# A routed FFN in slots of four blocks instead of two, and the last product scaled in its bank behind both branches

## The chip, the cores and the metric

One core of a Trainium2 chip runs the whole program. The metric is the device time of one execution in microseconds (us). TensorE (PE) does the matrix products, VectorE (DVE), ScalarE (ACT) and GpSimd (POOL) the rest, SyncE (SP) and POOL issue transfers. Each engine takes its instructions in program order.

## What is computed

Attention (4 batches, 8 heads, 768 tokens, each over its near neighbours and block summaries) gives x, 3072 rows of 512. Then each row goes through one of eight experts:

```
logits = x @ w_gate; local_gate = sigmoid(x @ w_local)
e = argmax(logits) if s == 0 or local_gate < 0.5 else the row before's e
p = softmax(logits)
out = p[e] * (max(x @ w1[e], 0) @ w2[e])      # w1 512x1024, w2 1024x512
```

## The kernel before

Rows are sorted by expert into 128-row blocks, numbered 0 to 25 here. With these inputs blocks 0 to 5 are batch 0 (one expert, known early, so they start while attention still runs), 6 to 16 belong to one expert (17 is empty), 18 to 23 to another, 24 to a third (25 is empty). Two "few" blocks of 32 rows take small rests of experts, in single fp32 products with unsplit weights ("raw").

A pair slot does two blocks. A gather on POOL fetches a block's rows, four transposes on PE and a cast and a subtraction on ACT and DVE (`tx`, `split_ps`) make xT in two parts, high and low, since each fp32 product is done as three matmuls on parts (high x high, high x low, low x high). Weights are split likewise, by ACT for the high part and DVE or POOL for the low part. Product 1 (`pair`, L1149 to L1151) is 96 matmuls of 256 columns, both blocks side by side; ACT and DVE make hT of it (L1155, L1157). Product 2 (`mm`, L1055 to L1057) is 48 matmuls of 512 columns, 24 for each block. In product 2 stand, at steps given by tables, the transposes of the next slot's blocks (PM0 in the first slot, PM in the others) and the splits of the next weights (PW1, PW2, four chunks each; SPLIT_BY says on which engine, V for DVE).

The order of each engine's work is the order of the code. Up to block 5, a list of small steps (the routing sort of batches 1 to 3) is dealt out between the steps of the slots by a planner (`flow`); whatever of it is left when the slot ends is put there. Two of its results matter here: the words that tell SP, POOL and the other engines which experts follow (PE L978), and the probabilities by block (`bp`: DVE L990 and three of L995, then 24 matmuls L999 on PE, then DVE L1002). Engines read words into registers with loads that their own sequencers run (`reg`, L1294), and branch on them. From block 14 on, each slot branches into a pair or a single. At block 22 a test on the number of blocks chooses the usual end (L1446) or a long one. The last product's rows are scaled by DVE and ACT, half each, and scattered (`last_rows`).

Of the kernel before, what the change touches and what calls it, by code (L numbers as in the profile page):

```python
# [19 lines left out]
P = 128  # L20
# [27 lines left out]
FEW_AT = 34  # L48
# [16 lines left out]
PM, PM0 = (2, 5), (10, 13)  # L65
# [12 lines left out]
class Kernel:  # L78
    def __init__(self, ctx, tc, qT, kT, vT, vW, maskc, identc, wgc, w1, w2, c32c, cb16c, out):
# [13 lines left out]
        self.turn = 0  # L93
# [44 lines left out]
    def bank(self, which):  # L138
        if which == "a" and "a2" in self.ps:
            self.turn ^= 1  # L140
            which = "a2" if self.turn else "a"
        return self.ps[which].tile([P, 512], F32, name="b" + which)
# [880 lines left out]

    def gather(self, i):
        t = self.xg[i % 2]
# [15 lines left out]
    def tx(self, i, half=0, bank="t"):  # L1041

        ps = self.transposes(lambda c: self.xg[i % 2][:, c, G9:G9 + P], bank).rearrange("p (k t) -> p k t", k=KT)
        self.split_ps(ps, self.xT[:, :, 0, half], self.xT[:, :, 1, half])

    def th(self, src, name):
        ps = self.transposes(lambda c: src[:, P * c:P * c + P], "t")
        h, l = [self.fw.tile([P, 512], F32R, name=name + x) for x in "hl"]
        self.split_ps(ps, h, l)
        return h, l  # L1050
# [8 lines left out]
    def store(self, yp, i, act=False, alone=False):  # L1059
        while self.have_p <= i:  # L1060
            self.small(1, True)
        if i >= LATE and (i % 2 or alone):
# [3 lines left out]
        y = self.mw2.tile([P, 512], F32, name="yo", bufs=2)  # L1066
# [17 lines left out]
    def few_rows(self, j):  # L1084

        t = self.xm[j]
        self.nc.gpsimd.indirect_dma_start(out=t.rearrange("p a d -> p (a d)"), out_offset=None, in_=self.x_rows,
                                          in_offset=bass.IndirectOffsetOnAxis(ap=self.gidx[0:FEW, SLOTS + j:SLOTS + j + 1], axis=0))

    def few_prep(self, j):  # L1090

        nc, fw, b = self.nc, self.fw, j
        i = SLOTS + j
        ps = self.bank("t")
        for c in range(KT):
            nc.tensor.transpose(out=ps[:, FEW * c:FEW * c + FEW], in_=self.xm[b][:, c, G9:G9 + P], identity=self.ident[0:FEW, 0:FEW])
        nc.vector.tensor_copy(out=self.xf[b].rearrange("p k t -> p (k t)"), in_=ps[:, 0:KT * FEW])
        rp = fw.tile([FEW, 2], F32, name="rp")
        nc.vector.tensor_copy(out=rp[:, 0:1], in_=self.sidx[0:FEW, i:i + 1])
        nc.vector.tensor_copy(out=rp[:, 1:2], in_=self.psort[0:FEW, i:i + 1])  # L1100
        yield
        ps = self.bank("t")
        nc.tensor.matmul(out=ps[:, 0:2], lhsT=self.four, rhs=rp, start=True, stop=True)
        nc.vector.tensor_scalar(out=self.idx4[b], in0=ps[:, 0:1], scalar1=4.0, scalar2=self.c["quad"], op0=ALU.mult, op1=ALU.add)
        nc.vector.tensor_copy(out=self.p4[b], in_=ps[:, 1:2])

    def few(self, j):

        nc, fw, b = self.nc, self.fw, j
        s1, s2 = self.raw  # L1110
        ps = self.bank("s")[:, 0:DF // 4]
        for k in range(KT):
            for q in range(4):
                c0 = 2 * P * (KT * q + k)
                nc.tensor.matmul(out=ps[FEW * q:FEW * q + FEW], lhsT=self.xf[b][:, k], rhs=s1[:, c0:c0 + DF // 4],
                                 start=(k == 0), stop=(k == KT - 1))
        h = fw.tile([P, DF // 4], F32, name="fh")
        nc.scalar.activation(out=h, in_=ps, func=AF.Relu)
        yield
        ps = self.bank("t")[:, 0:DF // 4]  # L1120
        for c in range(2):
            nc.tensor.transpose(out=ps[:, P * c:P * c + P], in_=h[:, P * c:P * c + P], identity=self.ident)
        hT = fw.tile([P, 2, 4, FEW], F32, name="fhT")
        nc.vector.tensor_copy(out=hT.rearrange("p c q t -> p (c q t)"), in_=ps)
        yield
        ps = self.bank("a")[:, 0:P]
        for f in range(FT):
            for q in range(4):
                c0 = f * DM + P * q
                nc.tensor.matmul(out=ps[FEW * q:FEW * q + FEW], lhsT=hT[:, f % 2, f // 2], rhs=s2[:, c0:c0 + P],  # L1130
                                 start=(f == 0), stop=(f == FT - 1))
        y = fw.tile([P, P], F32, name="fy")
        nc.vector.tensor_scalar(out=y, in0=ps, scalar1=self.p4[b], scalar2=None, op0=ALU.mult)
        nc.gpsimd.indirect_dma_start(out=self.out.rearrange("t (q d) -> (t q) d", q=4),
                                     out_offset=bass.IndirectOffsetOnAxis(ap=self.idx4[b], axis=0),
                                     in_=y, in_offset=None, bounds_check=4 * T_ALL - 1, oob_is_err=False)

    def pair(self, i, mid, w1, w2):

        nc = self.nc  # L1140
        xT, hT = self.xT, self.hT
        for f in range(0, FT, 2):
            ps = self.bank("s").rearrange("p (f t) -> p f t", f=2)
            for j in range(2):
                for k in range(KT):
                    c0 = 2 * P * (KT * (f // 2) + k) + P * j
                    xh, xl = [xT[:, k, part].rearrange("p h t -> p (h t)") for part in range(2)]
                    wh, wl = [w[0][:, c0:c0 + P] for w in (self.hi, self.lo)]
                    nc.tensor.matmul(out=ps[:, j], lhsT=wh, rhs=xh, start=(k == 0), stop=False)  # L1149
                    nc.tensor.matmul(out=ps[:, j], lhsT=wh, rhs=xl, start=False, stop=False)  # L1150
                    nc.tensor.matmul(out=ps[:, j], lhsT=wl, rhs=xh, start=False, stop=(k == KT - 1))  # L1151
                    if k % 2:
                        yield
            h, l = hT[:, f:f + 2, 0], hT[:, f:f + 2, 1]
            nc.scalar.activation(out=h, in_=ps, func=AF.Relu)  # L1155
            self.dve(0.6, self.t + 0.5)
            nc.vector.scalar_tensor_tensor(out=l, in0=ps, scalar=0.0, in1=h.bitcast(F32), op0=ALU.max, op1=ALU.subtract)  # L1157
        for half in range(2):
            yp = self.ya if half and 2 * i >= LATE else self.bank("a")
            s = slice(P * half, P * half + P)  # L1160
            for f in range(FT):
                self.mm(yp, hT[:, f, 0, s], hT[:, f, 1, s], 1, lambda t: t[:, f * DM:f * DM + DM], f == 0, f == FT - 1)
                yield
                j = FT * half + f
                pm = PM if i else PM0
                if j in pm:
                    mid(pm.index(j))
                for at, w in (PW1, w1), (PW2, w2):
                    if j in at and j < 2 * FT - 1:
                        w(*(q for q in range(4) if at[q] == j))  # L1170
            self.store(yp, 2 * i + half, 2 * i < EARLY)
            if half:
                w2(*(q for q in range(4) if PW2[q] == 2 * FT - 1))
        yield

    def single(self, i, mid, w1, w2):

        nc, fw = self.nc, self.fw
        hs = [fw.tile([P, 512], F32, name=f"hs{f}") for f in range(2)]

        def mm1(f, ks):
            for k in ks:
                if k == 0:
                    self.hp = self.bank("s")
                self.mm(self.hp.rearrange("p (a c) -> p a c", a=2), self.xT[:, k, 0, 0], self.xT[:, k, 1, 0], 0,
# [6 lines left out]
        hT = [self.th(hs[0], "h0"), None]  # L1192
# [10 lines left out]
        hT[1] = self.th(hs[1], "h1")  # L1203
        mm2((2, 3))
        for h in range(2):
            mid(h)
        w1(2, 3)
        mm2(range(4, 8))
        self.store(yp, i, alone=True)
        w2(0, 1, 2, 3)  # L1210

    def run(self):
# [54 lines left out]
        def block0():  # L1267
# [3 lines left out]
            self.xT = self.mw2.tile([P, KT, 2, 2, P], F32R, name="xT")  # L1271
            self.hT = self.mw2.tile([P, FT, 2, 2 * P], F32R, name="hT")
            for i in range(2):
# [3 lines left out]
                self.tx(i, i, "s")  # L1277
# [30 lines left out]
        def calls(n):  # L1308
# [19 lines left out]
            def mid(half):  # L1328
                if n < SLOTS:
                    while st["next"] <= n + half:  # L1330
                        self.small(1, True)
                    if half and n >= 2 * PAIRS:
                        with tc.If(reg(n + 1, (ENG.PE, ENG.Activation, ENG.DVE), 1) > 0):  # L1333
                            self.tx(n + half, half)
                    else:
                        self.tx(n + half, half)
                    freed()

            return mid, lambda *chunks: weights(0, n, chunks), lambda *chunks: weights(1, n, chunks)
# [11 lines left out]
        first = chain(block0(), self.pair(0, *calls(2)))  # L1351
# [5 lines left out]
        with ExitStack() as ctx:  # L1357
# [7 lines left out]
            self.xm = [fw.tile([FEW, NP, PW], F32, name=f"xm{i}") for i in range(2)]  # L1365
            self.xf = [fw.tile([P, KT, FEW], F32, name=f"xf{i}") for i in range(2)]
            self.idx4 = [fw.tile([P, 1], I32, name=f"idx4{i}") for i in range(2)]
            self.p4 = [fw.tile([P, 1], F32, name=f"p4{i}") for i in range(2)]
            self.four = fw.tile([FEW, P], F32, name="four")

# [7 lines left out]
            def few_part(some, part):  # L1378

                def run():  # L1380
                    with tc.If(some > 0):
                        next(part, None)

# [158 lines left out]
```

## Time and profile before

| | |
|---|---|
| median of three runs | 427.31 us (426.94 to 427.31) |
| profiled execution | 427.81 us, span on the core 425.9, outside it 1.9 |
| PE busy | 407.5 us, 96% of the span |
| mean granted TensorE clock | 0.995 |

Attention fills the first 119.8 us, the blocks the rest; the last matmul starts at 417.80. The span is what the instructions cover, the metric has 1.9 us more around it.

### The profile page before, as it was taken

To read this page: it belongs to the slowest core of one execution; us is meant where nothing else is said; L and a number is where in the kernel's file an instruction comes from. 1 tells how busy PE (TensorE), PEld (TensorE's weight loads), DVE (VectorE), ACT (ScalarE), POOL (GpSimd) and SP (SyncE) were. 2 spreads that over 40 slices of the span, in tenths; PEclk is the share of its full clock that TensorE was granted. 3 is DMA by queue.
4 is the path that set the end of the run, shared out by engine and by line. 5 is a ranking of instruction groups with operands and counts; after the bars stand their busy time and mean duration, and the time that the engine had idled before them with its cause. 6 is when DMAs were issued, how large, how long until landed. Compare 5 with 4: busy or idle time off the path is not lost. (4 is left out here: it accounts for less than half of the span.)

```text
span 425.9 us, 11477 instructions
## 1 busy us (share of the span) xinstructions
PE 407.5 (96%) x4216; PEld 352.3 (83%) x4216; DVE 225.0 (53%) x478; ACT 180.2 (42%) x423; POOL 195.2 (46%) x290
## 2 busy tenths in 40 slices
PE   7889999999999999999999999999999999999992
PEld 6668777778798898989879889898987998989771
DVE  4678979989696785774222312217321822222620
ACT  3879877778872221164201101117312820211640
POOL 5398767776587401266511200207730752020570
PEclk9999999999999999999999999999999999999998
DMA  8999999999590303918787600201951483020010
GB/s 295 415 408 408 407 403 413 399 414 368 153 335 0 106 2 121 373 49 311 291 345 266 241 29 3 85 25 47 332 183 54 178 299 101 13 83 27 3 52 31
DMA packets 21956, 85.89 MB, mean 202 GB/s; under 512 B 2638, under 2 KB 3152, under 8 KB 18800
## 3 DMA queue, kind: packets, MB, share of 16 engines
q1 hardware_dynamic: 17600, 70.46, 43.3%
q0 software_dynamic: 4128, 14.22, 9.9%
q8 instruction: 40, 0.66, 0.6%
q14 instruction: 44, 0.36, 0.3%
q10 hardware_dynamic: 144, 0.20, 0.2%
HBM read 71.40 MB, written 13.60 MB: 200 GB/s over the span
## 5 line engine op out<-in xcount | busy, mean ns | idle before, releaser
L1149 PE MATMUL bs<-xT,h 128*128 128x256 f32 x352 | 100.5, 285 | 0.0
L1150 PE MATMUL bs<-xT,h 128*128 128x256 f32 x352 | 99.8, 283 | 0.0
L1151 PE MATMUL bs<-xT,l 128*128 128x256 f32 x352 | 99.5, 283 | 0.0
L1155 ACT ACTIVATE hT<-bs 128x512 fp32r<-128x512 f32 x44 | 26.3, 597 | 111.0 <-PE bs L1151 109.3
L1055 PE MATMUL ba<-h,hT 128*128 128x512 f32 x176 | 71.6, 407 | 0.3 <-PEq L1333 0.2
L1149 PEld LDWEIGHTS bs<-xT,h 128*128 128x128 f32 x352 | 67.4, 192 | 1.7 <-issue 1.2
L1057 PE MATMUL ba<-h,hT 128*128 128x512 f32 x176 | 68.8, 391 | 0.0
L1056 PE MATMUL ba<-l,hT 128*128 128x512 f32 x176 | 68.8, 391 | 0.0
L1157 DVE SCALAR_TENSOR_TENSOR hT<-bs,hT 128x512 fp32r<-128x512 f32 x44 | 30.4, 690 | 72.7 <-ACT hT L1155 53.1
L1150 PEld LDWEIGHTS bs<-xT,h 128*128 128x128 f32 x352 | 67.5, 192 | 0.8 <-issue 0.5
L1151 PEld LDWEIGHTS bs<-xT,l 128*128 128x128 f32 x352 | 67.5, 192 | 0.0
L1027 POOL DMA_INDIRECT xg<-x_dram,gidx x26 | 29.9, 1151 | 70.7 <-PE bt L1038 30.3
L1081 POOL DMA_INDIRECT out_dram<-yo,sidx x22 | 24.8, 1127 | 73.6 <-ACT yo L1068 27.3
L346 ACT ACTIVATE pr<-bs,nm 128x120 f32<-128x120 f32 x192 | 52.0, 381 | 5.0 <-DVE nm L342 4.9
L1021 POOL TENSOR_TENSOR l<-stg,h 128x256 fp32r<-128x256 f32 x48 | 42.0, 907 | 21.3 <-ACT h L1013 21.1
L1057 PEld LDWEIGHTS ba<-h,hT 128*128 128x128 f32 x176 | 33.0, 188 | 7.4
L1055 PEld LDWEIGHTS ba<-h,hT 128*128 128x128 f32 x176 | 33.1, 188 | 6.9 <-ACTq L1323 0.5
L1056 PEld LDWEIGHTS ba<-l,hT 128*128 128x128 f32 x176 | 33.2, 189 | 5.6
L280 POOL COPY vw<-gs 24x444 f32<-24x444 f32 (+1 forms) x56 | 29.3, 550 | 18.4 <-issue 13.7
L1013 ACT CAST h<-stg 128x1024 fp32r<-128x1024 f32 x32 | 32.7, 1053 | 6.5 <-PE ba L1057 5.4
L367 PE MATMUL ba<-vw,pt 121*64 121x74 f32 x768 | 32.1, 231 | 1.3 <-POOL vw L280 0.8
L1016 DVE TENSOR_TENSOR l<-stg,h 128x1024 fp32r<-128x1024 f32 x20 | 26.6, 1339 | 12.0 <-ACT h L1013 10.4
(276 smaller groups left out, 629.5 us busy)
## 6 DMA issues: line engine op xcount, KB each, us to landing
stg<-in_w SPq DMA_DIRECT2D x16, 1024.0 KB, 7.4
vw<-in_vW SPq DMA_DIRECT2D x16, 888.0 KB, 9.9
raw<-in_w SPq DMA_DIRECT2D x8, 1024.0 KB, 9.8
x_dram<-xs SPq DMA_DIRECT2D x8, 876.0 KB, 9.0
kp<-in_kT SPq DMA_DIRECT2D x16, 384.0 KB
q<-in_qT SPq DMA_DIRECT2D x16, 384.0 KB, 11.2
vt<-in_vT SPq DMA_DIRECT2D x16, 384.0 KB, 10.5
wst<-in_w SPq DMA_DIRECT2D x8, 512.0 KB, 8.0
```

What stands on the lines that cost most here:

```text
L346: nc.scalar.activation(out=pr[:, h, u, :], in_=sp[:, h, u, :], func=AF.Exp, bias=nm[:, h, u:u + 1], scale=1.0)
L367: nc.tensor.matmul(out=ap[64 * c:64 * c + 64, u, h, :], lhsT=pt[0:W + 1, h, u, 64 * c:64 * c + 64], rhs=vw[n % NVW][0:W + 1, 2 * (NG * g + ...
L1013: self.nc.scalar.copy(out=hi, in_=src)
L1021: eng.tensor_tensor(out=lo[:, p], in0=src[:, p], in1=hi[:, p].bitcast(F32), op=ALU.subtract)
L1027: self.nc.gpsimd.indirect_dma_start(out=t.rearrange("p a d -> p (a d)"), out_offset=None, in_=rows, in_offset=bass.IndirectOffsetOnAxis(ap ...
L1055: nc.tensor.matmul(out=ps, lhsT=ah, rhs=wh, start=first, stop=False)
L1056: nc.tensor.matmul(out=ps, lhsT=ah, rhs=wl, start=False, stop=False)
L1057: nc.tensor.matmul(out=ps, lhsT=al, rhs=wh, start=False, stop=last)
L1149: nc.tensor.matmul(out=ps[:, j], lhsT=wh, rhs=xh, start=(k == 0), stop=False)
L1150: nc.tensor.matmul(out=ps[:, j], lhsT=wh, rhs=xl, start=False, stop=False)
L1151: nc.tensor.matmul(out=ps[:, j], lhsT=wl, rhs=xh, start=False, stop=(k == KT - 1))
L1157: nc.vector.scalar_tensor_tensor(out=l, in0=ps, scalar=0.0, in1=h.bitcast(F32), op0=ALU.max, op1=ALU.subtract)
```

## The change

Four blocks make a slot (`quad`): product 1 is then 96 matmuls of 512 columns for four blocks. Block pairs (2, 4) become one such slot, always; (6, 8), (10, 12) and (18, 20) become three, inside one branch (L1503 of the changed file) that these inputs take; its Else holds the old pairs. xT holds four blocks, four gather buffers serve them (two of them come free only after attention), the transposes of four blocks stand in each product 2 before a quad (PM0, PM4). The few blocks share one raw buffer that is reloaded between w1 and w2. The last product is scaled by DVE alone, behind both branches.

```diff
+FOURS = (6, 10, 18)
-PM, PM0 = (2, 5), (10, 13)
+PM, PM0, PM4 = (2, 5), (3, 6, 11, 14), (18, 21, 24, 27)
...
+    def buffer(self, i):
+        return i if i < 2 else (i - 2) % 4
...
     def last_rows(self):
-        y, h = self.yl, slice(256, 512)
-        self.nc.vector.tensor_scalar(out=y[:, 0:256], in0=self.ya[:, 0:256], scalar1=self.pl, scalar2=None, op0=ALU.mult)
-        self.nc.scalar.activation(out=y[:, h], in_=self.ya[:, h], func=AF.Copy, scale=self.pl)
-        self.scatter(y, self.il)
+        self.nc.vector.tensor_scalar(out=self.yl, in0=self.ya, scalar1=self.pl, scalar2=None, op0=ALU.mult)
+        self.scatter(self.yl, self.il)
...
+    def quad(self, i, *calls):
+
+        nc = self.nc
+        xh, xl = [[self.xT[:, k, part].rearrange("p h t -> p (h t)") for k in range(KT)] for part in range(2)]
+        for f in range(FT):
+            ps = self.bank("s")
+            for k in range(KT):
+                c0 = 2 * P * (KT * (f // 2) + k) + P * (f % 2)
+                wh, wl = [w[0][:, c0:c0 + P] for w in (self.hi, self.lo)]
+                nc.tensor.matmul(out=ps, lhsT=wh, rhs=xh[k], start=(k == 0), stop=False)
+                nc.tensor.matmul(out=ps, lhsT=wh, rhs=xl[k], start=False, stop=False)
+                nc.tensor.matmul(out=ps, lhsT=wl, rhs=xh[k], start=False, stop=(k == KT - 1))
                 yield
+            for h in range(2):
+                self.relu(ps[:, 2 * P * h:2 * P * h + 2 * P], *(self.hT[h][:, f, part] for part in range(2)))
+        yield from self.second(i, 4, *calls)
...
-            rest = chain(first, *(self.pair(i, *calls(2 * i + 2)) for i in range(1, EARLY // 2)))
+            rest = chain(first, self.quad(2, *calls(6, dict(zip(PM4, range(6, 10))))))
...
+            def few(j, part):
+                with tc.If(some[j] > 0):
+                    part(j)
+                    if part == self.few_1:
+                        few_load(j, 1)
+                    elif part == self.few_3 and j + 1 < FEWS:
+                        few_load(j + 1, 0)
...
+            other = 1 - reg(FOURS[-1] + 3, mybir.ALL_ENGINES, 1)
+            for i in FOURS:
+                other = other + reg(i + 2, mybir.ALL_ENGINES, 1)
+            for _ in range(6):
+                other = other + other
             kept = dict(st)
-            with tc.If(nb < LATE + 5 - EARLY) as usual:
-                slots(LATE, LATE + 4, LATE, LATE + 4)
+            with tc.If(nb + other < LATE + 5 - EARLY) as usual:
+                n = four(FOURS[1], four(FOURS[0]))
+                slots(2 * PAIRS, FOURS[2])
+                four(FOURS[2], n)
+                ends(LATE + 4, LATE, False)
```

Three places where rows move are shown. In the changed file the lines of unchanged code stand 3 to 33 further down.

DVE before, behind the sort's large steps and ahead of the last weight chunks of slot (4, 5); `bp` is the operand of the 24 matmuls, `l` the low part of a weight chunk:

```order
L995 TENSOR_TENSOR bp<-eqp,p_87 128x24x40
L1157 SCALAR_TENSOR_TENSOR hT<-bs,hT 128x2x256
L995 TENSOR_TENSOR bp<-eqp,p_87 128x24x40
L1157 SCALAR_TENSOR_TENSOR hT<-bs,hT 128x2x256
L995 TENSOR_TENSOR bp<-eqp,p_87 128x24x40
L1294 TENSOR_LOAD words
L1323 COMPARE_AND_BRANCH
L1016 TENSOR_TENSOR l_2481<-stg_2782,h_2479 128x1024
```

And in the changed kernel, DVE at the end of the slot of blocks 2 to 5:

```order
L1356 COMPARE_AND_BRANCH
L1019 TENSOR_TENSOR l_2482<-stg_2783,h_2480 128x1024
L1356 UNCONDITIONAL_BRANCH x2
L1356 COMPARE_AND_BRANCH
L1331 UNCONDITIONAL_BRANCH
L1356 UNCONDITIONAL_BRANCH
L998 TENSOR_TENSOR bp<-eqp,p_87 128x24x40
L1420 UNCONDITIONAL_BRANCH
L1005 TENSOR_REDUCE psort<-bt 128x40
```

The third step on `bp` stood ahead of all eight weight chunks; now it stands behind the last one that DVE splits.

PE before, from the last matmuls of block 5 to the next slot's product 1 (the 24 of L999 stand earlier, between matmuls of block 4):

```order
L1055 MATMUL ba_3472<-h_2480,hT 128x512
L1056 MATMUL ba_3472<-l_2482,hT 128x512
L1057 MATMUL ba_3472<-h_2480,hT 128x512
L1323 UNCONDITIONAL_BRANCH
L1294 TENSOR_LOAD words x2
L1149 MATMUL bs<-xT,h_2479 128x256
L1150 MATMUL bs<-xT,h_2479 128x256
```

And in the changed kernel, the last of the same 24 (now L1002), behind block 5's last matmul, and what follows:

```order
L1002 LDWEIGHTS A
L1002 MATMUL bt<-bp,A 128x120
L1420 UNCONDITIONAL_BRANCH
L1327 TENSOR_LOAD words x7
L1503 ISA
L1503 REGISTER_ALU
L1503 COMPARE_AND_BRANCH
L1200 MATMUL bs<-xT,h_2479 128x512
L1201 MATMUL bs<-xT,h_2479 128x512
```

All 24 matmuls moved behind the slot, and between them and the next product PE's sequencer has seven word loads and a branch instead of two loads.

PE before at the start of the second slot, from the last transposes (block 3):

```order
L1038 MATMUL bt<-ident,xg_110 128x128 x4
L1055 MATMUL ba_2841<-h_2480,hT 128x512
L1056 MATMUL ba_2841<-l_2482,hT 128x512
L1057 MATMUL ba_2841<-h_2480,hT 128x512
L1055 MATMUL ba_2841<-h_2480,hT 128x512
L1056 MATMUL ba_2841<-l_2482,hT 128x512
L1057 MATMUL ba_2841<-h_2480,hT 128x512
L1149 MATMUL bs<-xT,h_2479 128x256
```

And in the changed kernel (block 5, then the first quad):

```order
L1044 MATMUL bt<-ident,xg_2788 128x128 x4
L1062 MATMUL ba_2859<-h_2480,hT_2529 128x512
L1063 MATMUL ba_2859<-l_2482,hT_2529 128x512
L1064 MATMUL ba_2859<-h_2480,hT_2529 128x512
L1200 MATMUL bs<-xT,h_2479 128x512
L1201 MATMUL bs<-xT,h_2479 128x512
```

Three matmuls instead of six lie between the last transposes and the product that reads them.

## Rows read from the trace of the kernel before

**Rows 1.** The page: busy times of the span, slices of TensorE's clock.

```profile
PE 407.5 (96%) x4216; PEld 352.3 (83%) x4216; DVE 225.0 (53%) x478; ACT 180.2 (42%) x423; POOL 195.2 (46%) x290
...
PEclk9999999999999999999999999999999999999998
```

**Rows 2.** Windows: length, busy PE, PEld, DVE, ACT, POOL, then clock, DMA share, GB/s.

```profile
184.00:196.00 12.00, 12.00 (x81) 10.23 (x81) 8.42 (x10) 8.95 (x11) 11.11 (x9) 1.00 0.49 161
```

**Rows 3.** Timeline of TensorE: first and last of 9 products, then of 8.

```profile
241.12 0.40 PE L1057 MATMUL ba<-h,hT 128*128 128x512 f32 x1
243.17 0.39 PE L1057 MATMUL ba<-h,hT 128*128 128x512 f32 x1
...
275.61 0.28 PE L1149 MATMUL bs<-xT,h 128*128 128x256 f32 x1
276.56 0.28 PE L1151 MATMUL bs<-xT,l 128*128 128x256 f32 x1
```

**Rows 4.** Groups by line and timeline of the end, three engines.

```profile
L1071 DVE TENSOR_SCALAR yo<-ba,psort 128x512 f32<-128x512 f32 x16 | 12.0, 749 | 25.0 <-PE ba L1057 23.2 <-issue 1.8
...
418.30 0.48 DVE L1076 TENSOR_SCALAR yl<-ba,pl 128x256 f32<-128x256 f32 x1 [2.77 <-PE ba L1057]
418.87 0.47 ACT L1077 ACTIVATE yl<-ba,pl 128x256 f32<-128x256 f32 x1 [4.18 <-DVE yl L1076]
419.62 0.98 POOL L1081 DMA_INDIRECT out_dram<-yl,il  x1 [6.78 <-ACT yl L1077]
```

**Rows 5.** Timeline around the start of blocks 2 and 3, four engines.

```profile
143.06 0.60 PE L1038 MATMUL bt<-ident,xg 128*128 128x128 f32 x4
144.88 0.28 PE L1149 MATMUL bs<-xT,h 128*128 128x256 f32 x1
145.45 0.28 PE L1149 MATMUL bs<-xT,h 128*128 128x256 f32 x1
...
143.75 0.59 ACT L1031 CAST xT<-bt 128x512 fp32r<-128x512 f32 x1 [1.94 <-PE bt L1038]
...
144.37 0.69 DVE L1033 TENSOR_TENSOR xT<-bt,xT 128x512 fp32r<-128x512 f32 x1 [0.96 <-ACT xT L1031]
...
124.82 10.81 POOL L1021 TENSOR_TENSOR l<-wst,h 128x256 fp32r<-128x256 f32 x12 [1.59 <-ACT h L1013]
```

**Rows 6.** Gathers (L1027) and few's weights: least, median, most us to landing.

```profile
DMA to landing us min/median/max: 5.4/7.6/8.1
...
raw<-in_w SPq DMA_DIRECT2D x8, 1024.0 KB, 9.8
```

**Rows 7.** Timeline: gathers and transposes behind the routing words.

```profile
173.06 0.98 POOL L1027 DMA_INDIRECT xg<-x_dram,gidx  x1 [1.90 <-PE bs L1151]
...
183.49 0.60 PE L1038 MATMUL bt<-ident,xg 128*128 128x128 f32 x4
```

**Rows 8.** Timeline around the end of blocks 4 and 5; line L999.

```profile
182.91 1.15 DVE L995 TENSOR_TENSOR bp<-eqp,p 128x960 bf16<-128x960 f32 x1
194.52 1.28 DVE L1016 TENSOR_TENSOR l<-stg,h 128x1024 fp32r<-128x1024 f32 x1 [1.30 <-ACT h L1013]
...
194.56 0.28 PE L1149 MATMUL bs<-xT,h 128*128 128x256 f32 x1
...
L999 PE MATMUL bt<-bp,A x24: 216/216/226, 186.0 to 187.2; 128*128 128x120 bf16 x24
...
193.44 1.05 ACT L1013 CAST h<-stg 128x1024 fp32r<-128x1024 f32 x1 [0.31 <-PE ba L1057]
```

**Rows 9.** Line L1294 on TensorE's sequencer (PEldq), in two windows.

```profile
L1294 PEldq TENSOR_LOAD <-words x2: 309/400/492, 190.5 to 191.1; - x2
...
L1294 PEldq TENSOR_LOAD <-words x2: 300/302/305, 294.9 to 295.3; - x2
```

**Rows 10.** Windows behind the last matmul (418.2).

```profile
420.00:422.00 2.00, 0.00 (x0) 0.00 (x0) 0.00 (x0) 0.00 (x0) 0.60 (x1) 1.00 0.34 131
422.00:424.00 2.00, 0.00 (x0) 0.00 (x0) 0.00 (x0) 0.00 (x0) 0.00 (x0) 0.51 0.00 0
```

More of the change, by code (lines that the diff above doesn't have):

```diff
@@ new lines, in second @@
+    def second(self, i, blocks, mids, w1, w2):
+        for b in range(blocks):
+            late = i >= LATE and b == blocks - 1
+            yp = self.ya if late else self.bank("a", i < LATE)
+            s = slice(P * (b % 2), P * (b % 2) + P)
+            hT = self.hT[b // 2]
+            for f in range(FT):
+                self.mm(yp, hT[:, f, 0, s], hT[:, f, 1, s], 1, lambda t: t[:, f * DM:f * DM + DM], f == 0, f == FT - 1)
+                yield
+                j = FT * b + f
+                if j in mids:
+                    mids[j]()
+                k = j - FT * (blocks - 2)
+                for at, n, w in (PW1, k if i < EARLY else j, w1), (PW2, k, w2):
+                    if n in at and n < 2 * FT - 1:
+                        w(*(q for q in range(4) if at[q] == n))
+            self.store(yp, i + b, i < EARLY, late)
+        w2(*(q for q in range(4) if PW2[q] == 2 * FT - 1))
+        yield
@@ L1181, in mm1, with single @@
+    def single(self, i, mids, w1, w2):
+        nc = self.nc
+        at = (i - 2) % 4
+        hs = [self.lw.tile([P, 512], F32, name=f"hs{f}") for f in range(2)]
         def mm1(f, ks):
@@ L1326, in weights, with turn @@
                         refill(w, nxt)
[L1328 to L1339, printed above, removed]
+            def turn(u):
+                while st["next"] <= u:
+                    self.small(1, True)
+                if u % 2 and u >= 2 * PAIRS:
+                    with tc.If(reg(u, (ENG.PE, ENG.Activation, ENG.DVE), 1) > 0):
+                        self.tx(u)
+                else:
+                    self.tx(u)
+                freed()
+            mids = {j: lambda u=u: turn(u) for j, u in mids.items() if u < SLOTS}
+            return mids, lambda *chunks: weights(0, n, chunks), lambda *chunks: weights(1, n, chunks)
         def tick(G, point):
@@ L1349, in tick @@
                 f(*args)
-        first = chain(block0(), self.pair(0, *calls(2)))
+        first = chain(block0(), self.pair(0, *calls(2, dict(zip(PM0, range(2, 6))))))
         for G, i in START:
@@ L1376, in run, with few_load @@
             self.have_words = have_words
[L1378 to L1382, printed above, removed]
[L1384 to L1386 removed]
+            def few_load(j, w):
                 e = reg(COLS + SLOTS + j, (ENG.SP,), E - 1)
                 with tc.If(reg(SLOTS + j, (ENG.SP,), 1) > 0):
[L1389 to L1394 removed]
+                    for h in range(2):
+                        p = slice(2048 * h, 2048 * h + 2048)
+                        self.fetch(self.raw[:, p], w, p.start, p.stop, e)
+            rest = chain(first, self.quad(2, *calls(6, dict(zip(PM4, range(6, 10))))))
             while self.steps:
@@ L1411, in run @@
-                steps[n + 26], steps[n + 29] = [lambda g=g: next(g, None) for g in [self.few_prep(j)] * 2]
-                part = few_part(some[j], self.few(j))
-                for k in range(3):
-                    steps[n + FEW_AT + 2 + 4 * k] = part
-            steps[FEW_AT + 12] = lambda: few_load(1)
-            for i in range(EARLY // 2, PAIRS):
-                for n, _ in enumerate(self.pair(i, *calls(2 * i + 2))):
-                    steps.pop(n + FEW_AT * (i - EARLY // 2), int)()
@@ L1419, in run @@
-            assert not steps, steps
+                for n, part in zip(FEW_AT[j], (self.few_rows, self.few_turn, self.few_index)):
+                    steps[n] = lambda j=j, part=part: part(j)
+                for n, part in zip(FEW_AT[j][3:], (self.few_1, self.few_2, self.few_3)):
+                    steps[n] = lambda j=j, part=part: few(j, part)
+            def run(gen, n0=0):
+                n = n0
+                for n, _ in enumerate(gen, n0):
+                    steps.get(n, int)()
+                return n + 1
@@ new lines, in slots, with slot @@
+            def slots(i0, i1, n=0):
+                for i in range(i0, i1, 2):
+                    c = i, i + 2, dict(zip(PM, (i + 4, i + 5)))
+                    if i < 2 * PAIRS:
+                        n = run(self.pair(i, *calls(*c[1:])), n)
+                    else:
+                        slot(*c)
+            def slot(i, *c):
+                two = reg(i + 1, mybir.ALL_ENGINES, 1)
+                kept = dict(st)
+                with tc.If(two > 0) as full:
+                    for _ in self.pair(i, *calls(*c)):
+                        pass
+                st.update(kept)
+                with full.Else():
+                    self.single(i, *calls(*c))
@@ L1426, in slots, with ends @@
+            nc.vector.memset(self.ya, 0.0)
+            def ends(i1, sure, more):
                 with ExitStack() as c:
-                    for i in range(i0, i1, 2):
-                        n = i + 2 if i + 2 < most else SLOTS
+                    for i in range(LATE, i1, 2):
                         if i >= sure:
```

198 lines of the change are left out of this document (87 added, 111 removed).

## The prediction

> **What bounds the kernel now.** I read the page first, for who is busy: TensorE 96% of the span, every other engine 53% or less, and TensorE's clock at its full level in all but the last slice [rows 1]. So TensorE's own stream sets the time, and a window must say whether it also does where the change works. At the end of blocks 4 and 5 it was busy for 12.00 of 12.00 us, at granted clock 1.00, while DVE had 8.42, ACT 8.95 and POOL 11.11 [rows 2]. A change can win here only by giving TensorE less to do, and it loses each time that TensorE is made to wait. I then read the timeline for the price of one matmul, by the distance from start to start, since durations overlap: with 512 columns nine steps took 2.05 us, 0.228 each; with 256 columns, 0.95 us lie between the first and the ninth start, eight steps of 0.119 [rows 3]. Half the columns cost 52% of the time. About 0.010 us of a matmul is paid whatever its width.
>
> **What the wider product saves.** A quad replaces 192 matmuls of 256 columns by 96 of 512: 192 x 0.119 = 22.85 against 96 x 0.228 = 21.9. That is 0.96; with 0.120, which the two-digit starts allow as well, it is 1.15. I take 1.1 for each of the four quads: **-4.4**, bounds -3.8 and -4.6. Product 2 keeps its matmuls. ACT and DVE get twice as many instructions of half the width for hT; they are idle for a quarter of the time or more [rows 2] and half a product (2.7 us, 12 matmuls) lies between one f and the next, so I take nothing. If this cover were gone, the two product-1 banks would stall TensorE at each f.
>
> [...]
>
> **The end.** Before, DVE scaled its half from 418.30, ACT began the other at 418.87 and ended it at 419.34, and POOL's scatter began at 419.62 [rows 4]. One DVE instruction of 512 columns of this kind takes 0.749 [rows 4], so it ends at 418.30 + 0.75 = 419.05: **-0.3** (bounds 0 and -0.3).
>
> **The start of the first quad.** Before, block 3's transposes began at 143.06, ACT's cast 0.69 later (143.75, 0.59 long), DVE's subtraction at 144.37, ending at 145.06; product 1 began at 144.88 and its first three matmuls took 0.57 instead of 0.36, so 0.21 were lost to the low part [rows 5]. Now only three matmuls, 0.68, lie behind the transposes instead of six. Relative to the nominal start the low part is ready 0.68 later, at 145.06 - 144.88 + 0.68 = 0.86 after it, and the second matmul wants it at 0.23. That costs 0.63, against 0.21: **+0.5** with rounding up for the cast, which is late by some 0.1 as well. The gathers of blocks 4 and 5 now go out behind POOL's long split, which ends at 124.82 + 10.81 = 135.63 [rows 5]; they land 5.4 to 8.1 us after issue [rows 6], the second one (about 1 us after the first) at 142.0 to 144.7. Its transposes want it about 0.7 before the start of product 1, near 143.7. Bounds 0.3 to 1.5.
>
> **Block 6's rows.** The words come a little later, as the sort's steps are dealt between longer slots; I estimate 2 us from counting the steps ahead of them. Before, the first gather behind the words was issued at 173.06 and its transposes ran at 183.49, 10.4 later [rows 7]; landing takes up to 8.1 [rows 6]. So the slack of 2.3 is used up, within a fraction: **+0.3**, bounds 0 and 1.2.
>
> **The stall at the end of the first quad.** The third step on `bp` ran at 182.91 for 1.15 before, done two us ahead of the 24 matmuls L999 at 186.0, which were covered by other matmuls on both sides [rows 8]. Now DVE has it behind the last weight chunk that it splits. That chunk can't be early: its cast waits for product 2 (ACT at 193.44), and its subtraction ran from 194.52 to 195.80, while the next product began at 194.56 [rows 8]. Call the end of block 5's last matmul step E. Then the chunk is split at E + 1.24, the third step ends 1.15 later, at E + 2.39, and the 24 matmuls, which stand at E in TensorE's stream now, wait until then: **+2.4**. Behind them in TensorE's queue stands the whole next quad, so nothing covers it; ACT and POOL wait for that quad in turn. Bounds 1.9 (the chunk's subtraction and its cast somewhat earlier) and 2.9 (one more late transpose of block 8 or 9 ahead of them). I see no reason for a gain.
>
> **The words behind it.** The 24 matmuls start 1.2 us apart from first to last, 0.052 each, in both kernels [rows 8]. Behind them the sequencer has seven word loads and a branch. Before, the two loads of the next slot began at 190.5 [rows 9], 4.06 us ahead of the product at 194.56 [rows 8]: TensorE's sequencer ran 4.06/0.228 = 18 matmuls ahead and no further. One load follows another after 0.4 to 0.6 [rows 9], seven take 2.9, and an estimate of 0.4 covers the branch and the arithmetic. While TensorE waits for `bp`, the sequencer can pass 18 of the 24 and stands. The loads begin when six matmuls have run, 18 x 0.052 = 0.94 before the last one is issued; the quad follows 2.9 + 0.4 - 0.94 = 2.4 after the last: **+2.4**. Bounds 0 (the sequencer gets past all 24 in the wait) and 3.7 (0.6 for each load).
>
> [...]
>
> **Edits at nothing.** The two branches on `two` of blocks 18 and 20 vanish, with their loads; they ran ahead of TensorE's work. The few blocks have the same matmuls at other steps. Their second weights now wait for the first to be used, 21 steps of 0.68 or 14.4 us before they are wanted; a load landed after 9.8 in the median [rows 6]. If they are late, TensorE waits in the middle of a quad.
>
> **Sum.** -4.4 - 0.3 + 0.5 + 0.3 + 2.4 + 2.4 = +0.9, against the profiled 427.81: 428.7. That execution was 0.5 above the median of 427.31, so I forecast **428.2**, slower by 0.2%, just about what a measurement of this kernel can tell from no change (0.2%, 0.85 us). By its own bounds it lies between 427.3 and 429.2.
>
> **Rivals.**
> 1. The sequencer gets past the 24 matmuls while TensorE waits, and the second stall is gone: 428.2 - 2.4 = 425.8, faster. It decides if the lead is counted other than in matmuls, since these are a quarter as long as those by which I measured it. For it: rows 9 show a lead, not its limit. Against it: 18 matmuls with their weight loads are 36 instructions, and the 24 with theirs are 48.
> [...]
> [...]
> 4. Few's weights come late, three reloads in a row, each by a us or less: 429.5. It decides if a load takes over some 13 us.
>
> **Chances.** The forecast 0.48; rival 1 0.20; rival 2 0.13; rival 3 0.05; rival 4 0.07; something that gains more than I see 0.07. Of the forecast's 0.48 its own range puts 0.26 above 428.16 and 0.22 within 0.2%. Slower: 0.26 + 0.13 + 0.05 + 0.07 = 0.51; same: 0.22 + 0.02 of rival 1 = 0.24; faster: 0.18 + 0.07 = 0.25. The range holds rivals 1, 2 and 4 with their bounds, 425.5 to 430.9, and leaves out about 0.16.
>
> **What would show it.** In the changed profile: starts of product 1 in a quad 0.228 apart, 21.9 us for each; two idle stretches of TensorE of 2.4 us on both sides of the 24 matmuls, the first released by DVE's `bp`, the second by TensorE's own sequencer; the second matmul of the first quad 0.6 late; the last scatter 0.3 nearer to the last matmul. The forecast is wrong if the sequencer's loads lie inside the first stall, if the clock is under 1.00 after it, or if the quad's starts are closer to 0.24 apart.

## The result and the profile after

| | before | changed |
|---|---|---|
| median, us | 427.12 (426.90 to 427.31, 4 runs) | 431.38 (430.87 to 431.74, 4 runs) |
| ratio | 1 | 1.0099, 95% interval 1.0082 to 1.0116 |
| profiled execution, its span | 427.81, 425.9 | 431.03, 429.1 |
| mean granted TensorE clock | 0.995 | 0.988 |

Slower by 1.0%, where I forecast slower by 0.2%: outside the range, on the forecast's side. The two profiled spans differ by 3.2 only, because attention took 1.0 longer in the one of before: block 0's first product began at 119.75 there and at 118.72 after. From that start to the end of the span it is 306.15 against 310.38, a loss of 4.2 that agrees with the medians. By the starts of the first matmul of each slot in the two timelines, it falls like this:

| blocks | before | after | change |
|---|---|---|---|
| 0, 1 | 25.13 | 26.10 | +0.97 (the transposes of 4 and 5 stand here now) |
| 2 to 5 | 49.68 | 55.66 | +5.98 |
| 6 to 13 | 104.41 | 104.41 | 0.00 |
| 14 to 17 | 36.57 | 36.37 | -0.20 |
| 18 to 21 | 46.71 | 45.55 | -1.16 |
| 22 to the last matmul | 35.55 | 34.55 | -1.00 (no transposes are left for here) |
| from the last matmul's start | 8.10 | 7.74 | -0.36 |

One slot loses more than the whole. The page of the changed kernel (busy times; TensorE's clock in 40 slices) already points to the place: besides the last slice, which is at 8 in [rows 1] too, one slice in the middle is at 6:

```profile
PE 406.1 (95%) x3832; PEld 333.3 (78%) x3832; DVE 230.4 (54%) x510; ACT 184.3 (43%) x453; POOL 194.0 (45%) x290
...
PEclk9999999999999999996999999999999999999998
```

The windows around it (columns as in [rows 2], which had 12.00 busy of 12.00 and clock 1.00):

```profile
184.00:196.00 12.00, 9.90 (x49) 7.76 (x48) 9.75 (x10) 9.88 (x13) 9.02 (x7) 1.00 0.25 72
196.00:200.00 4.00, 2.10 (x24) 1.84 (x24) 0.99 (x2) 0.00 (x0) 3.34 (x4) 0.57 0.98 396
200.00:205.00 5.00, 4.52 (x14) 3.67 (x15) 0.58 (x3) 0.07 (x1) 3.35 (x5) 0.66 0.99 358
```

TensorE was idle for 2.1 of 12 us, then busy for 2.1 of 4, and the granted clock was 0.57 and 0.66. Its timeline names the stalls:

```profile
193.51 0.40 PE L1064 MATMUL ba<-h,hT 128*128 128x512 f32 x1
196.00 2.10 PE L1002 MATMUL bt<-bp,A 128*128 128x120 bf16 x24 [2.10 <-DVE bp L998]
200.48 0.77 PE L1200 MATMUL bs<-xT,h 128*128 128x512 f32 x1 [2.38 <-issue]
201.05 0.63 PE L1201 MATMUL bs<-xT,h 128*128 128x512 f32 x1
203.18 0.50 PE L1200 MATMUL bs<-xT,h 128*128 128x512 f32 x1
203.52 0.39 PE L1201 MATMUL bs<-xT,h 128*128 128x512 f32 x1
```

The last matmul of block 5 starts at 193.51, so the next could start at 193.74. The 24 matmuls L1002 wait for DVE's `bp` until 196.00, 2.26 later, and the second quad starts at 200.48. Its first step takes 0.57 and the next five 0.43 each, instead of 0.228, at a granted clock of 0.50 (window from 200.48 to 203.00); after 203.18 a step is 0.34, then 0.23 again. In DVE's timeline the last weight chunk and the third step on `bp` stand as the order had them (before, the step was at 182.91, [rows 8]):

```profile
193.65 1.23 DVE L1019 TENSOR_TENSOR l<-stg,h 128x1024 fp32r<-128x1024 f32 x1 [1.20 <-ACT h L1016]
194.79 1.15 DVE L998 TENSOR_TENSOR bp<-eqp,p 128x960 bf16<-128x960 f32 x1
```

And TensorE's sequencer began the seven word loads only at 196.3, behind the first stall, and the last one at 199.1 [rows 9 had two, ahead of the work]:

```profile
L1327 PEldq TENSOR_LOAD <-words x7: 305/311/602, 196.3 to 199.1; - x7
```

In the same view they have between 0.31 and 0.60 each. Two smaller waits stand earlier, the low part of block 5's xT at the start of the first quad (0.72 and 0.34 to the next start instead of 0.228; [rows 5]) and block 6's rows behind the words ([rows 7]):

```profile
144.82 0.50 PE L1200 MATMUL bs<-xT,h 128*128 128x512 f32 x1
145.54 0.50 PE L1201 MATMUL bs<-xT,h 128*128 128x512 f32 x1 [0.23 <-DVE xT L1039]
145.88 0.39 PE L1202 MATMUL bs<-xT,l 128*128 128x512 f32 x1
...
181.49 0.40 PE L1064 MATMUL ba<-h,hT 128*128 128x512 f32 x1
182.83 0.66 PE L1044 MATMUL bt<-ident,xg 128*128 128x128 f32 x4 [0.94 <-DMA xg<-x_dram,gidx]
```

The end is shorter, as forecast: from the last matmul's start to the scatter 1.45, against 1.82 before (417.80, and 419.62 in [rows 4]).

```profile
421.36 0.39 PE L1064 MATMUL ba<-h,hT 128*128 128x512 f32 x1
...
422.81 0.98 POOL L1086 DMA_INDIRECT out_dram<-yl,il  x1 [6.37 <-DVE yl L1082]
```

### The profile page after: what moved, and what is told of

Its sections match the earlier page's. It is cut to its first block, busy times and chain, and to the rows that moved or that the text cites. A ratio compares the mean times of both kernels' runs of the same rounds, so it can differ in the third digit from the quotient of the medians.

```text
span 429.1 us, 10640 instructions
## 1 busy us (share of the span) xinstructions
PE 406.1 (95%) x3832; PEld 333.3 (78%) x3832; DVE 230.4 (54%) x510; ACT 184.3 (43%) x453; POOL 194.0 (45%) x290
## 5 line engine op out<-in xcount | busy, mean ns | idle before, releaser
L1062 PE MATMUL ba<-h,hT 128*128 128x512 f32 x192 | 78.1, 407 | 0.3
L1168 ACT ACTIVATE hT<-bs 128x256 fp32r<-128x256 f32 (+1 forms) x76 | 31.8, 419 | 101.8 <-PE bs L1202 53.4
L1064 PE MATMUL ba<-h,hT 128*128 128x512 f32 x192 | 75.3, 392 | 0.0
L1063 PE MATMUL ba<-l,hT 128*128 128x512 f32 x192 | 75.2, 392 | 0.0
L1170 DVE SCALAR_TENSOR_TENSOR hT<-bs,hT 128x256 fp32r<-128x256 f32 (+1 forms) x76 | 35.4, 465 | 70.9 <-ACT hT L1168 70.9
L1200 PE MATMUL bs<-xT,h 128*128 128x512 f32 x128 | 51.2, 400 | 2.4 <-issue 2.4
L1201 PE MATMUL bs<-xT,h 128*128 128x512 f32 x128 | 50.5, 394 | 0.2 <-DVE xT L1039 0.2
L1202 PE MATMUL bs<-xT,l 128*128 128x512 f32 x128 | 50.3, 393 | 0.0
L1062 PEld LDWEIGHTS ba<-h,hT 128*128 128x128 f32 x192 | 36.1, 188 | 8.3 <-issue 1.9
L1064 PEld LDWEIGHTS ba<-h,hT 128*128 128x128 f32 x192 | 36.1, 188 | 8.3
L1037 ACT CAST xT<-bt 128x512 fp32r<-128x512 f32 x22 | 12.8, 588 | 66.2 <-PE bt L1044 66.1
L370 PEld LDWEIGHTS ba<-vw,pt 121*64 121x64 f32 x768 | 27.2, 136 | 6.4 <-issue 3.8
L1200 PEld LDWEIGHTS bs<-xT,h 128*128 128x128 f32 x128 | 24.4, 191 | 8.5 <-issue 3.0
```

Of the source, the lines that this page charges most:

```text
L370: nc.tensor.matmul(out=ap[64 * c:64 * c + 64, u, h, :], lhsT=pt[0:W + 1, h, u, 64 * c:64 * c + 64], rhs=vw[n % NVW][0:W + 1, 2 * (NG * g + ...
L1062: nc.tensor.matmul(out=ps, lhsT=ah, rhs=wh, start=first, stop=False)
L1063: nc.tensor.matmul(out=ps, lhsT=ah, rhs=wl, start=False, stop=False)
L1064: nc.tensor.matmul(out=ps, lhsT=al, rhs=wh, start=False, stop=last)
L1168: self.nc.scalar.activation(out=h, in_=ps, func=AF.Relu)
L1170: self.nc.vector.scalar_tensor_tensor(out=l, in0=ps, scalar=0.0, in1=h.bitcast(F32), op0=ALU.max, op1=ALU.subtract)
```

## Experiments

Each time below is a ratio to before on the same chip, with its 95% interval.

**1. The sort's step earlier.** In the loop over the first quad, the planner's step (it says how much time a step of the slot takes) is larger, so that more of the sort is dealt out per step.

```diff
             while self.steps:
                 next(rest, None)
-                self.flow(C_T)
+                self.flow(0.70)
```

Expected: 

> The changed kernel with the planner's step in the loop over the first quad at 0.70 us instead of 0.65, so that the third step on bp and the 24 matmuls of the probabilities come between the steps of the quad's second product. Theory (two stalls of 2.3 and 2.5 us, and a fall of the clock between them that costs 2.0): all three go, since the word loads then lie within the sequencer's lead of about 4 us; 431.4 - 6.8 = 424.6, granted clock 1.00 from 190 to 210. Rival 1 (the matmuls behind the stalls are slow through the weight transfers of that time, not through the clock): 426.6. Rival 2 (the sort's step is wanted by something else and its wait comes back in the quad): 428 or more.

Measured: 422.68 us, ratio 0.9908 (0.9892 to 0.9925). Two windows of the place, busy throughout at clock 1.00:

```profile
190.00:195.00 5.00, 5.00 (x25) 3.82 (x24) 3.27 (x4) 3.84 (x6) 4.04 (x4) 1.00 0.83 278
195.00:200.00 5.00, 5.00 (x24) 4.14 (x23) 1.51 (x6) 1.66 (x4) 3.42 (x5) 1.00 1.09 404
```

Both stalls and the slow matmuls are gone, from one number in the planner, and the clock stayed at 1.00 at a DMA share of 1.09. The time fell further than expected: block 6's rows came in time, too, and 0.8 us of a gap in few's second product (below) did not occur. One new wait appeared, 0.8 for the routing words, whose product TensorE reached too early:

```profile
160.47 0.39 PE L1202 MATMUL bs<-xT,l 128*128 128x512 f32 x1
161.64 0.32 PE L981 MATMUL bt<-ident,w 128*1 128x46 f32 x4 [0.79 <-DVE words L984]
```

**2. The word loads ahead of the quad's end.** The seven loads move into the loop, some steps ahead of its end; the sums stay.

```diff
+            def all_loads():
+                st["some"] = [reg(SLOTS + j, mybir.ALL_ENGINES, 1) for j in range(FEWS)]
+                st["nb"] = reg(2 * COLS, mybir.ALL_ENGINES, SLOTS)
+                st["o"] = [reg(i, mybir.ALL_ENGINES, 1) for i in (FOURS[-1] + 3, *(i + 2 for i in FOURS))]
```

Expected: 

> The changed kernel with the seven word loads of the branch put three steps ahead of the end of the first quad; bp stays late. Theory: the first stall of 2.3 stays, the second (2.5) goes. If the clock falls after the first stall alone, 431.4 - 2.5 = 428.9; if it takes both stalls to bring it down, 426.9. Rival (the second stall is not the loads but the branch or code behind it): 431.4, second stall unchanged.

Measured: 428.22 us, ratio 1.0038 (1.0023 to 1.0052).

```profile
192.28 0.40 PE L1064 MATMUL ba<-h,hT 128*128 128x512 f32 x1
196.79 2.31 PE L1002 MATMUL bt<-bp,A 128*128 128x120 bf16 x24 [4.11 <-DVE bp L998]
198.86 0.78 PE L1200 MATMUL bs<-xT,h 128*128 128x512 f32 x1
```

The second stall is gone: the quad follows the 24 matmuls, 2.07 after their start. So it was the loads. The first one grew from 2.1 to 4.1 idle, because ACT and DVE run the same loads: ACT ran its seven from 189.9 to 192.2 and began its last two casts at 192.41 (at 191.62 in the changed kernel, though product 2 ended 1.2 sooner here), and DVE's last chunk, which needs the second of them, began at 194.44 after 3.21 idle (193.65 in the changed kernel). So little is won in the place itself: from the start that the product behind block 5 could have had to the quad it is 198.86 - 192.51 = 6.35, against 200.48 - 193.74 = 6.74. The spans of the two profiles are 3.1 apart because product 2 ended 1.2 sooner, fewer matmuls of the quad ran slow (0.6) and few's gap (below) is absent (0.8); that the time came near the 428.9 expected is luck. The clock fell in this kernel with the first stall alone (0.71 from 195 to 200, 0.95 from 200 to 205).

**3. More loads, no wait for `bp`.** Experiment 1 with 15 loads; the eight added cancel out in the sum.

```diff
+            for i in range(4):
+                other = other + reg(SLOTS, mybir.ALL_ENGINES, 1) - reg(SLOTS, mybir.ALL_ENGINES, 1)
```

Expected: 

> The first experiment's kernel with 15 word loads instead of 7 ahead of the branch. Theory (the sequencer runs 18 matmuls, 4.1 us, ahead and no further): 15 x 0.41 + 0.4 = 6.5 us of loads stick out by 2.4, TensorE idles that long before the first matmul of the second quad, 2.4 above the first experiment. [...]

Measured: 428.84 us, ratio 1.0054 (1.0036 to 1.0073).

```profile
194.06 0.40 PE L1064 MATMUL ba<-h,hT 128*128 128x512 f32 x1
198.08 0.47 PE L1200 MATMUL bs<-xT,h 128*128 128x512 f32 x1 [3.63 <-issue]
198.39 0.40 PE L1201 MATMUL bs<-xT,h 128*128 128x512 f32 x1
199.14 0.63 PE L1201 MATMUL bs<-xT,h 128*128 128x512 f32 x1
```

```profile
L1327 PEldq TENSOR_LOAD <-words x15: 305/311/497, 190.6 to 196.8; - x15
```

The loads began at 190.6, 3.7 us ahead of the start that the quad could have had (194.06 + 0.23). In that time stand 17 matmuls, 13 wide ones and four short transposes, so that the lead is as long in matmuls as before and shorter in time. The loads started 0.44 apart, and with the branch they took until 198.08, 7.5 us; TensorE was idle for 3.6, more than the 2.4 expected, as the lead was shorter and the loads and the branch longer than assumed. What holds the sequencer at 17 or 18 matmuls no run here shows. The clock fell here as well, behind a single stall, and only after three full-speed matmuls of the quad (0.90 from 195 to 200, 0.76 from 200 to 205).

**4. The first stall filled.** Ten matmuls whose result is not read stand between block 5's last product and the 24.

```diff
+                if count == 81:
+                    ps = self.bank("s")
+                    for _ in range(10):
+                        nc.tensor.matmul(out=ps, lhsT=self.hi[0][:, 0:P], rhs=self.hi[0][:, 0:512], start=True, stop=True)
                 self.flow(C_T)
```

Expected: 

> The changed kernel with ten matmuls of 512 columns, of which nobody reads the result, between the last matmul of the first quad and the 24 matmuls that wait for bp: 2.3 us of work that ends when bp does. Both waits stay as long as they were, but TensorE idles in the second one alone. Theory (idling brings the clock down): the granted clock stays at 1.00 and the time falls by the clock's cost, 431.4 - 2.0 = 429.4. Rival (slow through the transfers of that time): 431.4, the first matmuls of the second quad still 0.43 apart.

Measured: 429.71 us, ratio 1.0077 (1.0061 to 1.0094).

```profile
192.65 2.44 PE L1433 MATMUL bs<-h 128*128 128x512 f32 x10
194.93 1.43 PE L1002 MATMUL bt<-bp,A 128*128 128x120 bf16 x24
199.32 0.47 PE L1200 MATMUL bs<-xT,h 128*128 128x512 f32 x1 [2.95 <-issue]
199.62 0.39 PE L1201 MATMUL bs<-xT,h 128*128 128x512 f32 x1
200.78 0.40 PE L1200 MATMUL bs<-xT,h 128*128 128x512 f32 x1
```

```profile
195.00:200.00 5.00, 2.05 (x28) 1.83 (x28) 0.98 (x5) 0.00 (x0) 4.36 (x6) 1.00 0.95 369
200.00:205.00 5.00, 5.00 (x24) 4.10 (x23) 0.85 (x2) 0.77 (x2) 2.92 (x4) 1.00 1.02 371
```

The clock stayed at 1.00 and the quad's first starts are 0.30 and then 0.23 apart, at a DMA share of 1.02: it was the clock that made them slow, not the transfers. The time fell by 0.2% of before and not by the expected 2.0 us; from block 5's end to the quad's seventh start, 200.78 - 192.65 = 8.13 stand against 203.18 - 193.74 = 9.44 in the changed kernel, a gain of 1.3. The 0.7 that the 24 matmuls save at full clock (1.43 busy, against 2.10) is not won: from the first of the loads behind them to the quad it is 4.0 (195.3 to 199.32), against 4.2 in the changed kernel. All this is one execution, the fastest of four (428.19). The other three took 429.50 to 430.92, the slowest of them at a mean clock of 0.986, as low as the changed kernel's 0.987 to 0.988; so filling the stall did not keep the clock up each time, and the median says little on its price.

**5, 6. The step's place in the kernel before.** The same line of the old kernel with 0.60, which puts the third step on `bp` behind DVE's last chunk there too, and with 0.70.

Expected with 0.60: 

> The kernel before, with the planner's step in the loop over the first slots at 0.60 instead of 0.65: the third step on bp falls behind DVE's last weight chunk and the 24 matmuls behind block 5's last product, as in the changed kernel, but with pairs and with two word loads behind them. Theory (the stall belongs to the place of the step, not to quads): TensorE waits some 2.3 us for bp, the two loads lie inside the 24 matmuls, the clock stays up; 2.3 slower than before. Rival (a pair's slot hides it): same as before.

Measured: 429.96 us, ratio 1.0071 (1.0053 to 1.0089).

```profile
194.75 1.89 PE L999 MATMUL bt<-bp,A 128*128 128x120 bf16 x24 [2.15 <-DVE bp L995]
196.40 0.56 PE L1149 MATMUL bs<-xT,h 128*128 128x256 f32 x1
196.76 0.41 PE L1150 MATMUL bs<-xT,h 128*128 128x256 f32 x1
```

Pairs have the same stall when the step is late, 2.15, and no second one, since two loads fit. The expectation missed the clock (0.66 from 195 to 200): the first twelve or so matmuls were 0.21 apart instead of 0.12, and product 1 took 12.7 instead of 11.5. The profiled execution was the slowest of four (431.48, mean clock 0.990); another of them, with the same stall in its order of work, took 429.67 at a mean of 0.997. That is some 2.6 us at half clock in all, an estimate from 0.3% of 428, less than the 3.4 us that this fall lasted in the profiled one (195.5 to 199.0), so the clock hardly fell there.

Expected with 0.70: 

> The kernel before with the planner's step at 0.70, as in the first experiment. Theory (before has no stall there, so nothing to win): same as before within 0.5. Rival (the first experiment won by a better spread of the sort's steps as such): 1 us or more faster than before, and so much less of the first experiment's gain is due to quads.

Measured: 426.83 us, ratio 1.0008 (0.9998 to 1.0017). No change: experiment 1's gain over before is not the planner's.

**7. Quads in the branch undone.** Experiment 1 with `slots(EARLY, LATE)` in the branch in place of the three quads.

Expected: 

> The first experiment's kernel with the three quads in the branch undone: pairs for blocks 6 to 13 and 18 to 21, the quad of blocks 2 to 5 stays. Theory (each quad saves 96 fixed costs, 1.2 us): 3.6 slower than the first experiment, about 0.3 us faster than before. Rival (half or more of the first experiment's gain comes from elsewhere, as the moved transposes): 1.8 or less slower than the first experiment.

Measured: 425.25 us, ratio 0.9967 (0.9956 to 0.9979). In the timelines, blocks 6 to 13 take 104.47 (193.60 to 298.07) against 102.23 in experiment 1 (193.76 to 295.99), and 18 to 21 take 46.67 against 45.55: 1.12 for each quad, 3.4 for three. The profiled spans are 3.0 apart (423.0 and 420.0) and the ratios 0.6%, 2.5 us, so the whole agrees with the place to within a microsecond.

**8. Transposes one step earlier.** Experiment 1 with PM0 = (3, 6, 10, 13).

Expected: 

> The first experiment's kernel with the transposes of blocks 4 and 5 one step (0.68 us) earlier, at steps 10 and 13 instead of 11 and 14. Theory: the second matmul of the first quad waits 0.5 less, 0.5 faster than the first experiment. Rival (the gathers of blocks 4 and 5, which go out behind POOL's split, have not landed): the wait moves to the transposes, same or slower.

Measured: 422.97 us, ratio 0.9912 (0.9893 to 0.9932), in the time the same as experiment 1. In the trace the wait is gone: first and third start of the quad are 0.51 apart, where the changed kernel has 1.06.

```profile
144.31 0.40 PE L1200 MATMUL bs<-xT,h 128*128 128x512 f32 x1
144.82 0.39 PE L1202 MATMUL bs<-xT,l 128*128 128x512 f32 x1
```

**9. The last rows in halves.** Experiment 1 with `last_rows` as it was.

Expected: 

> The first experiment's kernel with the last product's rows scaled by DVE and ACT, half each, as before the change. Theory: the last scatter begins 0.3 later behind the last matmul, 0.3 slower than the first experiment, which the profile shows and the time hardly. Rival: no difference in the profile either.

Measured: 425.23 us, ratio 0.9947 (0.9931 to 0.9963). Here (first fence) and in experiment 1 (second), the last scaling on DVE and the scatter:

```profile
415.26 0.48 DVE L1083 TENSOR_SCALAR yl<-ba,pl 128x256 f32<-128x256 f32 x1 [2.70 <-PE ba L1064]
...
416.53 0.99 POOL L1088 DMA_INDIRECT out_dram<-yl,il  x1 [6.63 <-ACT yl L1084]
```

```profile
412.62 0.75 DVE L1082 TENSOR_SCALAR yl<-ba,pl 128x512 f32<-128x512 f32 x1 [2.75 <-PE ba L1064]
...
413.65 0.99 POOL L1086 DMA_INDIRECT out_dram<-yl,il  x1 [6.21 <-DVE yl L1082]
```

From DVE's start to the scatter, 1.27 against 1.03: the edit is worth 0.24. The time lies above experiment 1's by far more than that, by 0.4% in the ratios and by 2.9 us between the two profiled executions. Their traces put 0.8 of the 2.9 on the gap in few's product and 1.4 on attention (block 0 began at 118.91 here, at 117.55 there), neither of which this edit touches. The whole time therefore does not show the edit's worth; the place does.

**10. Both small waits removed.** Experiment 1 with 0.67 and PM0 = (3, 6, 10, 13).

Expected: 

> The first experiment's kernel with a planner's step of 0.67 and the transposes of blocks 4 and 5 at steps 10 and 13. Theory: the wait for the routing words (0.8 in the first experiment) is gone, the first quad waits 0.5 less; if block 6's rows still land in time, 1 us faster than the first experiment, 421.7 to 422.0. Rival: later words make block 6's rows late again (1.1 in the changed kernel), no gain.

Measured: 423.18 us, ratio 0.9895 (0.9883 to 0.9908), the lowest ratio of all. The product of the words no longer waits, nor does the quad's second matmul:

```profile
163.24 0.32 PE L981 MATMUL bt<-ident,w 128*1 128x46 f32 x4
...
144.70 0.40 PE L1200 MATMUL bs<-xT,h 128*128 128x512 f32 x1
144.94 0.44 PE L1201 MATMUL bs<-xT,h 128*128 128x512 f32 x1
...
193.36 0.47 PE L1200 MATMUL bs<-xT,h 128*128 128x512 f32 x1
```

From the first quad's start to the second's it is 193.36 - 144.70 = 48.66, against 50.06 in experiment 1: 1.4 faster in the place, while the ratios of the two kernels overlap. Block 6's rows did not wait.

**11. The changed kernel again.** Expected: 

> The changed kernel once more, beside the two above on one chip. Theory: 4 us slower than before again, with the stalls of 2.3 and 2.6 and the slow matmuls behind them in the profile; the gap of 0.6 in the few block's second product (seen once in the changed kernel's profile, in no experiment) does not come back if it was chance. Rival: it comes back, and few's weights are late in this kernel.

Measured: 431.62 us, ratio 1.0098 (1.0081 to 1.0114), with the same stalls, but the clock fell later and cost more:

```profile
196.00 1.43 PE L1002 MATMUL bt<-bp,A 128*128 128x120 bf16 x24 [2.10 <-DVE bp L998]
200.18 0.76 PE L1200 MATMUL bs<-xT,h 128*128 128x512 f32 x1 [2.74 <-issue]
200.74 0.63 PE L1201 MATMUL bs<-xT,h 128*128 128x512 f32 x1
...
205.18 0.40 PE L1200 MATMUL bs<-xT,h 128*128 128x512 f32 x1
```

The 24 matmuls ran at full speed here (1.43 busy, against 2.10 in the first profile), and the clock was down from about 198.0, in the second stall. The quad's first twelve steps took 5.00 us, against 4.19 in the first profile (200.48 to 204.67) and 2.84 at full clock (experiment 4): the fall cost 2.2 here and 1.3 there, in the same kernel.

The gap in few's second product came back: 64 matmuls took 2.68, as they did (2.68 to 2.72) in experiments 9 and 10 and in the changed kernel's first profile, while they took 1.88 in experiments 1 to 4, 7 and 8. No edit separates the kernels that have it from those that do not, and the changed kernel had it both times. TensorE's own sequencer ends it in the profile, so late weights are not shown; what it is stays open.

## Why the prediction was wrong

- **The gain of wide products: right.** Forecast 1.1 for a quad, measured 1.12 (experiment 7).
- **The end: right.** -0.3 forecast, 0.24 by itself (experiment 9), 0.36 in the change.
- **The start of the first quad: right.** +0.5 forecast; the first two steps took 1.06 instead of 0.46, the one ahead of them 0.37 instead of 0.23, and before lost 0.21: +0.53. Moving the transposes gave it back (experiment 8).
- **The stall for `bp`: right** in place, cause and size: 2.4 forecast, 2.26 measured; moving the step alone removes it (experiment 1), and it comes with the step in the old kernel (experiment 5).
- **The words behind it: right cause, undersized.** Forecast 2.4. From 196.00 to 200.48 it is 4.48, against 1.25 for the 24 matmuls in experiment 1: 3.2. The lead of 18 matmuls held: the loads began 0.3 us into the 24. From the first load to the quad it is 4.2, where the sum had 3.3: the seven starts lie 2.8 apart from first to last, near the forecast, but from the last one to the quad it is 1.4 (199.1 to 200.48; 197.9 to 199.32 in experiment 4). The 0.4 for the branch and the arithmetic in that stretch was an estimate of mine, which no run shows. Rival 1 is refuted by the second stall itself and by where the loads began; experiment 3 has a lead of 17 without a wait ahead of it.
- **Block 6's rows: undersized.** +0.3, bounds to 1.2; from 181.49 to 182.83 it is 1.34 instead of 0.23, +1.1. No experiment changed this alone.
- **The clock: the step that failed.** The sum priced both stalls as idle time alone and left the fall of the clock to rival 2, at 0.13. One sign that the prediction named for being wrong, a clock under 1.00 behind the stall, came. In the changed kernel's first profile it fell behind a wait of 2.10 us, during the 24 matmuls (1.00 from 196.0 to 196.5, 0.50 from 197.0 to 203.0); in experiment 5 it fell there too, behind 2.15, and in experiment 11 in the second stall, of 2.74. Its price was 1.3 in the profiled execution (experiment 4), where six matmuls of the quad ran slow, and 2.2 in experiment 11, where ten did. The [rows 10], where the clock held for 3.8 us of idling, are one execution of one idling: in experiment 3's trace the clock was down 2.0 us after the last matmul (last section).
- **The gap in few's product: not foreseen,** +0.8. Rival 4 had named a late weight at this place; the experiments do not show that, and the cause stays open.
- **The range: too narrow for its own terms.** The prediction gives 427.3 to 429.2 by its bounds, and 425.5 to 430.9 with three rivals. Its upper end has 2.5 for the clock, which no run shows; 1.3 and 2.2 were measured. Added up as they stand, the bounds of the terms reach from 2.7 below 427.3 to 5.5 above it, 424.6 to 432.8, and the measured 431.38 lies inside. Rivals were taken one at a time, with the other terms at their middle.

Together: four quads -4.4 (2 x -1.12, -1.16, and about -1.0 for the first, as its slot without these waits has it in experiment 10, 48.66 against 49.68), the end -0.4, the quad's start +0.5, block 6 +1.1, `bp` +2.3, the words +3.2, the clock +1.3, few +0.8, blocks 14 to 17 -0.2: +4.2, as measured, though each term is good to 0.2 only. The sum had +0.9. Of the difference the clock is 1.3, the words, block 6 and few 0.8 each. Each loss but few's gap was in the sum or a rival with its cause, and they came together.

## What to carry to other kernels

When a slot gets longer, look at what the order puts at its end: work that a planner dealt out between its steps can pile up there, behind the last thing that the longer slot waits for, and one number in the planner moved 8 us here. Count what a sequencer must run between two products, word loads above all, against the lead that it has in the trace; when a wait takes the lead away, the loads stand open, as the seven did here, with TensorE idle for 2.38 us. Price an idle stretch of TensorE with the slow matmuls behind it, as a cost that comes in some executions and not in others (1.3 and 2.2 us in two of the changed kernel here, none in the profiled one of experiment 4). And when several losses can come together, add their bounds.

## What the runs showed of the hardware

- When the granted clock falls differs from execution to execution. Behind the last matmul of the kernel TensorE idled to the end of the span, 7.7 us in the trace of before and 7.4 in the changed kernel's first one. There the clock was at half from 420.90 at the latest in experiment 3, 2.0 us after that matmul ended (418.88), and still at 1.00 up to 420.00 in experiment 7, 4.8 us after it (415.16); in [rows 10] it held for 3.8. Experiment 3 first:

```profile
420.90:422.90 2.00, 0.00 (x0) 0.00 (x0) 0.00 (x0) 0.00 (x0) 0.07 (x1) 0.50 0.35 131
```

```profile
418.00:420.00 2.00, 0.00 (x0) 0.00 (x0) 0.00 (x0) 0.00 (x0) 0.00 (x0) 1.00 0.33 123
```

- In these runs, then, a stall of 2 to 4 us sometimes brought the clock down and sometimes did not. It fell behind 2.15 us without a matmul and some of the 24 narrow ones (experiment 5) and behind 3.6 us (experiment 3), and stayed at 1.00 through 2.95 us of idling in the profiled execution of experiment 4. Whether the matmuls ahead of that idling helped is not shown.
- Half clock lasted until 203.4 in the changed kernel's first profile and until 204.9 in experiment 11, 2.9 and 4.7 us of the quad.
- At its word loads TensorE's sequencer was 18 matmuls ahead before (4.06 us, [rows 8, 9]) and 17 in experiment 3 (3.7 us). In the changed kernel's first profile it began them 0.3 us after the first of the 24 that had waited for `bp` (196.3 and 196.00).
- From the first of seven word loads on TensorE's sequencer to the quad behind their branch it was 4.2 us in the changed kernel's first profile (196.3 to 200.48) and 4.0 in experiment 4 (195.3 to 199.32).
- Attention's length varied by up to 2.4 us between profiled executions of kernels whose edits lie behind it (block 0's first matmul at 117.40 to 119.75): edits under 1 us are read from their place in the trace here, not from the whole.
